# A new hand-written order for a fused attention and token-mixing kernel: narrow tiles for most q transposes and k'v products, and eps of 14 groups added by TensorE

## The chip, the cores and the metric

One core of a Trainium2 chip runs the whole kernel. The metric is device time in microseconds, the median of several runs. The profile is one further execution taken by the hardware profiler; its span runs from the first to the last instruction.

## What is computed

Linear attention with cosine weights, then a token mixer, for 8 batches, 8 heads, 576 tokens and head width 64, all inputs and the output in float32:

```python
r = np.maximum(x, 0.0)                                     # phi, for q and for k
phi = np.concatenate([r * c, r * s], axis=-1)              # c, s: cos and sin by token
kv = einsum('bhsf,bhsd->bhfd', k_p, v); z = sum(k_p, axis=2)
x = einsum('bhsf,bhfd->bhsd', q_p, kv) / (einsum('bhsf,bhf->bhs', q_p, z)[..., None] + 1e-06)
...
wq = x @ w_q; wk = x @ w_k                                 # x: 8 x 576 x 512, heads side by side
mixed = einsum('bst,btd->bsd', einsum('bsd,btd->bst', wq, wk) / 8, x)
out = np.maximum(mixed, 0.0) @ w_out
```

The kernel never forms the 576 x 576 token matrix: it computes wk'x (64 x 512) first and multiplies that by wq.

## The kernel before

The unit of the first half is H, one of 16: half a batch, four heads, as two pairs of heads. A step is a small function; its name is two letters and its number is H, a group g (two to an H), a batch b, or an output block. What happens to one H:

- LK, LQ, LV (line 145) load k, q and v from memory, mostly in two halves of 288 KB ("a" and "b", one per pair of heads), into rings of five raw buffers each. All loads and all stores are issued by SP, in the order written.
- RK and RQ (lines 203 and 205) take the relu and cast to bfloat16. V is scaled by the cosine and sine tables into buffer v2 (tiles named v) on one of two routes: VG (line 248) does it in one pass on POOL from the raw data; or CV (lines 209, 211, 213) casts it on some engine and VS (line 234) multiplies on DVE. Two v2 buffers exist, so that v of H waits for the k'v product of H-2.
- QT transposes q on PE. Wide (line 295) takes nine transposes of 128 x 128, narrow (line 301) eighteen of 64 x 64. QM then multiplies by the table on DVE: two instructions for wide (line 316), one for narrow (line 320). QT_WIDE names the H's that are wide.
- KV multiplies k by v2 on PE: wide (line 275) in eighteen matmuls, narrow (line 285) in thirty-six that use 64 x 64 tiles. KV_WIDE names the wide ones. KE copies the result out of PSUM (lines 209 or 213).
- N (line 340) multiplies q by k'v for a group g: numerator and denominator. The eps is added either by EP, on ACT (line 357) or DVE (line 359), or, for a group in EPS_PE, by two tiny matmuls (line 348); then RC reads the denominator straight from PSUM (line 378). RC or RJ (line 381) is the reciprocal, X (line 393) the division into x, on DVE.
- XT (line 406) or XR (line 419) transposes x on PE, with full or with half-height tiles, and XE copies it out.

The second half goes by batch b: WK, WQ, KX (lines 439, 452, 466), their copies KW, QW, XK, two copies of kx across partitions (XA, XB), the products MX (line 489) with relu ME (lines 500, 502). Two batches together give nine output blocks WO (line 509, four matmuls of 128 x 128 by 128 x 512), copied by OE into one of sixteen o buffers and stored by ST (line 519). The weights come by LW and are cast by CW.

Nothing schedules this at run time: ORDER, a string of words, is the program. A word is a step, with `@A`, `@V` or `@G` for the engine (ACT, DVE, POOL) and `:n` for its PSUM bank or its o buffer. Each engine works through its own words in the order written and waits where its data or its buffer is not ready. PSUM has eight banks, which the words share out. The loads of an H may run at most five H's ahead of the relus and the scaling.

Of the kernel before, what the change touches and what calls it, by code (L numbers as in the profile page):

```python
# [31 lines left out]
RC6 LQ4a KX0:4 X6 RK2@A QT2:2 RC7 X7 CV5@A KV2:0 LK7a XK0@V LV4a QM2 XB0@G QW0@A XT3:6 LV4b KE2@A
RK5@A LK4a VS5a N5:0 WU5:2 LK4b N4:2 VS5b XE3@A RQ5@G LV7a EP5@V KV5:4 RC5 RC4 X5 XA0@A LV7b X4
QT5:6 KE5@A RQ4@G LQ7b MX0:0 QM5 XR2:2 ME0@A LQ7a QT4:4 XE2@A LQ6a N10:0 QM4 MX1:6 CV4@G LK7b EP10@A
ME1@A WK1:2 LV6b WQ1:3 RC10 KW1@A VS4 RK4@A LQ6b KX1:2 MX2:6 LW2 N11:4 XK1@V QW1@A ME2@A EP11@V
KV4:2 LK6b RC11 XA1@G X10 CV7a@A CV7b@G LK6a X11 MX5:6 MX4:0 KE4@A RQ7b@G LV6a RQ7a@A VS7 N8:2 N9:4
ME5@A LV8a ME4@A QT7:6 RK7@G LW3 EP8@V EP9@V RJ4 RQ6a@A XT5:0 X8 LW4 XB1@G XE5@A X9 KV7:2 LW5 RQ6b@G
# [6 lines left out]
OE4:5@A KV8:0 QM8 XB2@A KV9:6 ST4 KE8@A LV12a MX9:4 KE9@A MX11:0 VG11a N16:2 ME9@A LK10a ME11@V
WQ3:6 RC16 LQ10b KX3:7 X16 QW3@A MX10:0 LV10a XK3@A N17:4 ME10@A N19:2 RK11@V N18:6 LV10b EP19@A
WO11:0 EP17@V RQ11@A LQ12a RC17 EP18@V X17 WO5:1 VG11b OE11:6@V WO10:4 OE5:5@A RC19 RC18 ST11 X18
WO9:5 LK12a X19 LK10b QT11:6 LQ13b OE9:7@A RQ10@G LV12b KV11:2 XA3@A QM11 XR8:0 LK12b KE11@A XR9:6
VG10a XE8@A QT10:2 LQ12b XE9@V WO0:5 QM10 OE10:8@A MX13:0 OE0:6@A MX12:6 N22:2 WO12:4 RQ13a@G ME12@V
EP22@A LV15a XB3@A ME13@A LV13a RC22 VG10b WK4:5 X22 LQ14b LV14b MX14:0 KW4@A N23:6 ME14@V LQ14a
MX15:2 EP23@A KX4:5 RK10@A LV13b WQ4:0 XK4@V RQ13b@G RC23 WO3:1 ME15@A X23 XA4@G XB4@A QW4@A RQ12b@G  # L50
KV10:2 OE3:9@V RQ12a@A QT13:6 OE12:10@A VG12 MX18:0 WO14:5 QM13 KE10@A ST12 ME18@A LK13b XR11:2
OE14:11@A LK13a MX16:0 N21:6 XE11@V ME16@A LV14a N20:4 EP21@A EP20@V RK12@A QT12:0 RJ10 X21 WO16:2
RQ14b@A X20 WO13:3 QM12 VG13 XR10:4 OE13:10@A MX19:6 KV12:0 ME19@A ST13 WO17:3 OE16:12@A LK15b
KE12@V XE10@V LK14b MX17:0 LK14a OE17:13@A N25:6 ME17@V N24:4 LV15b RQ14a@A WK5:3 ST2 EP25@V EP24@V
RK13@A RJ12 QT14:0 X24 WO21:2 KW5@A X25 CV14a@G KV13:4 OE21:10@A QM14 CV14b@A WQ5:3 ST21 KE13@A
# [6 lines left out]
ST14 XR15:0 ST6 MX25:4 MX27:6 XE15@V ME25@A WO22:3 ST23 ME27@V ST1 WK7:0 OE26:9@V ST24 MX24:6 KW7@A
MX26:4 WQ7:1 ME24@A ME26@V ST19 KX7:0 OE22:8@V ST26 WO28:2 XK7@A QW7@V ST22 XA7@G WO27:3 OE28:11@A
XB7@G ST28 MX31:0 MX28:4 MX30:6 ME31@V ME28@A WO29:2 ME30@A OE27:7@V MX29:4 OE29:4@V WO30:0 ME29@A
ST27 ST29 WO32:1 OE30:2@V WO33:4 ST30 OE32:9@V WO34:0 ST32 OE33:8@A WO35:1 ST33 OE34:7@V WO31:4 ST34
OE35:4@A ST35 OE31:2@A ST31
# [532 lines left out]
```

## Time and profile before

| | |
|---|---|
| runs | 119.72, 120.26, 120.61 us; median 120.26 |
| span of the profiled execution | 117.9 us, 4967 instructions |
| PE, DVE, ACT, POOL busy | 96.3, 91.0, 82.7, 64.8 us |
| moved by DMA | 39.38 MB, mean 334 GB/s over the span |
| loads | 96 of k, q and v, 6 of weights; 36 stores |

The profiled execution gives its span alone, so that is set beside the runs: 2.4 us of the median lie before the first and after the last instruction. Busy time counts a matmul to its modelled end, and matmuls overlap, so PE's 96.3 us is more than its queue's own pace needs. A row of a group reads: line, engine, operation, output and inputs with shapes, count, then busy time and mean length of one in ns, then idle time just ahead and what ended it. In the chain of waits a row is start, length, and what the time went to.

### The profile page before, as it was taken

How to read it: one execution, taken by the hardware profiler on the slowest of the kernel's cores; microseconds unless marked ns; L12 is line 12 of the kernel's file. 1: busy time of each engine (PE TensorE's matmuls, PEld its weight loads, DVE VectorE, ACT ScalarE, POOL GpSimd, SP SyncE). 2: the span in 40 equal slices, each digit the busy share in tenths (PEclk: the TensorE clock that was granted, in tenths of full speed). 3: DMA queues.
4: the chain of work that ended last, by engine and by line, in shares of the span. 5: the costliest groups of instructions: out<-in, count | busy, mean ns of one | idle time of the engine just before them, and what ended most of it. 6: DMA issues, size and time to landing. Idle time of an engine off the chain costs nothing.

```text
span 117.9 us, 4967 instructions
## 1 busy us (share of the span) xinstructions
PE 96.3 (82%) x2109; PEld 65.3 (55%) x2109; DVE 91.0 (77%) x163; ACT 82.7 (70%) x146; POOL 64.8 (55%) x66
## 2 busy tenths in 40 slices
PE   0007866887897879998999889997999999999970
PEld 0006855756676768546966556654784566463420
DVE  2009799699899998989798887796997996794620
ACT  4555578489999797997684769975888783546340
POOL 7600599843435984584599972899549921102000
PEclk9999999999999999999999999999999999999998
DMA  3999999999999999999999899786989456999874
GB/s 95 353 389 408 393 363 351 391 389 396 385 393 389 391 385 387 389 395 384 387 381 341 271 317 379 274 253 215 299 285 321 171 205 268 402 343 402 340 306 172
DMA packets 20662, 39.38 MB, mean 334 GB/s; under 512 B 3232, under 2 KB 3232, under 8 KB 20640
## 3 DMA queue, kind: packets, MB, share of 16 engines
q1 hardware_dynamic: 20640, 39.07, 91.8%
q8 instruction: 16, 0.26, 1.0%
q14 instruction: 6, 0.05, 0.1%
HBM read 29.62 MB, written 9.44 MB: 331 GB/s over the span
## 4 chain that ended last, share of the span: by engine, by line
PE 46%; DMA 25%; DVE 9%; SPq 8%; ACT 4%; issue 3%; POOL 2%; POOLq 0%; DVEq 0%
PE ps L509 23%; DMA kraw<-in_k_dram 11%; DMA vraw<-in_v_dram 9%; SPq L145 8%; DMA qraw<-in_q_dram 5%; DVE qm L316 5%; PE ps L340 4%; PE ps L452 3%; PE ps L466 3%; PE ps L489 3%; PE ps L439 3%; PE ps L285 3%; PE ps L419 2%; PE ps L295 2%; POOL rq L205 2%
## 5 line engine op out<-in xcount | busy, mean ns | idle before, releaser
L248 POOL TENSOR_TENSOR v<-vraw,vtab 128x1152 bf16<-128x1152 f32 (+1 forms) x12 | 35.6, 2976 | 4.5 <-DVE qm L316 2.5
L509 PE MATMUL ps<-wow,mix 128*128 128x512 bf16 x144 | 34.6, 380 | 0.0
L393 DVE TENSOR_TENSOR x<-ps,rec 128x640 bf16<-128x640 f32 x32 | 25.4, 816 | 0.7
L209 ACT COPY o<-ps 128x512 f32<-128x512 f32 x25 | 14.6, 590 | 10.5 <-PE ps L509 9.2
L316 DVE TENSOR_TENSOR qm<-ps,qtab 128x1152 bf16<-128x1152 bf16 x28 | 19.7, 749 | 1.3 <-PE ps L295 1.2
L509 PEld LDWEIGHTS <-mix 128*128 128x128 bf16 x144 | 12.5, 98 | 14.5 <-issue 1.7
L295 PE MATMUL ps<-ident,rq 128*128 128x128 bf16 x126 | 10.3, 232 | 10.9 <-ACT rq L203 10.0
L234 DVE TENSOR_TENSOR v<-vb,vtab 128x2304 bf16<-128x2304 bf16 (+1 forms) x11 | 12.0, 1110 | 7.5 <-ACT vb L209 6.7
L500 ACT ACTIVATE mix<-ps 128x576 bf16<-128x576 f32 x23 | 14.5, 651 | 2.5 <-PE ps L489 2.3
L340 PE MATMUL ps<-kvs,qm 64*128 64x65 bf16 x640 | 14.0, 193 | 2.8 <-DVE qm L316 1.8
L340 PEld LDWEIGHTS <-qm 64*128 64x128 bf16 x640 | 12.6, 96 | 4.9 <-issue 3.3
L295 PEld LDWEIGHTS <-rq 128*128 128x128 bf16 x126 | 8.2, 104 | 12.5 <-issue 9.9
L203 ACT ACTIVATE rk<-kraw 128x1152 bf16<-128x1152 f32 (+1 forms) x14 | 13.9, 995 | 0.5 <-DMA kraw<-in_k_dram 0.3
L211 POOL TENSOR_SCALAR kx<-kx 64x256 bf16<-64x256 bf16 x10 | 4.0, 400 | 15.8 <-ACT kx L209 10.1
L205 POOL TENSOR_SCALAR rq<-qraw 128x576 bf16<-128x576 f32 (+1 forms) x13 | 10.1, 776 | 4.4 <-ACT rk L203 2.6
L211 POOL TENSOR_SCALAR vb<-vraw 128x576 bf16<-128x576 f32 (+1 forms) x7 | 5.7, 809 | 10.8 <-DMA vraw<-in_v_dram 9.5
L285 PE MATMUL ps<-v,rk 64*64 64x130 bf16 x432 | 9.1, 228 | 1.9 <-ACT mix L500 0.7
L209 ACT CAST kvs<-ps 128x260 bf16<-128x260 f32 (+1 forms) x15 | 6.5, 436 | 5.1 <-PE ps L285 3.8
L285 PEld LDWEIGHTS <-rk 64*64 64x64 bf16 x432 | 7.5, 112 | 4.3 <-ACT mix L500 1.3
L502 DVE TENSOR_SCALAR mix<-ps 128x576 bf16<-128x576 f32 x9 | 6.8, 753 | 3.3 <-PE ps L489 3.1
L213 DVE COPY xT<-ps 128x1280 bf16<-128x1280 bf16 (+1 forms) x9 | 7.3, 813 | 2.2 <-PE ps L419 2.0
L203 ACT ACTIVATE rq<-qraw 128x576 bf16<-128x576 f32 (+1 forms) x10 | 8.3, 830 | 0.9 <-DMA qraw<-in_q_dram 0.8
(65 smaller groups left out, 135.0 us busy)
## 6 DMA issues: line engine op xcount, KB each, us to landing
kraw<-in_k_dram SPq DMA_DIRECT2D x32, 288.0 KB, 5.9
qraw<-in_q_dram SPq DMA_DIRECT2D x32, 288.0 KB, 5.9
vraw<-in_v_dram SPq DMA_DIRECT2D x32, 288.0 KB, 5.9
out_dram<-o SPq DMA_DIRECT2D x36, 256.0 KB, 3.0
wof<-in_moe_w_out_dram SPq DMA_DIRECT2D x4, 256.0 KB, 5.7
wkf<-in_moe_w_k_dram SPq DMA_DIRECT2D x1, 128.0 KB, 6.7
wqf<-in_moe_w_q_dram SPq DMA_DIRECT2D x1, 128.0 KB, 6.5
```

Of the source, the lines that this page charges most:

```text
L203: A.activation(dst, s, AF.Relu)
L205: eng.tensor_scalar(dst, s, FMAX, 0.0, op0=ALU.min, op1=ALU.max)
L209: A.copy(dst, s)
L234: V.tensor_mul(v2_b[H % NV2][:, part, :, :, 0:D], vb_b[H % NPREP][:, part].unsqueeze(3).to_broadcast([P, n, C, 2, D]), vtab.unsqueeze(1).t ...
L248: G.tensor_mul(dst[:, part, :, :, 0:D], s[:, part].unsqueeze(3).to_broadcast([P, n, C, 2, D]), vtab.unsqueeze(1).to_broadcast([P, n, C, 2, ...
L285: nc.tensor.matmul(kv_v[o, r, :], rk_of(H)[a, pr, c, :], v2_b[H % NV2][a, pr, c, :, 0:D + 1], start=(c == 0), stop=(c == C - 1))
L295: nc.tensor.transpose(qt_v[:, c, :], rq_b[H % NPREP][:, c, :, :], ident)
L316: V.tensor_mul(qm_b[H % NQM][:, :, r, 0:C, :], q_t[:, r].unsqueeze(1).to_broadcast([P, 2, C, H2]), qtab)
L340: nc.tensor.matmul(nv[:, pr, u, :], qm_b[H % NQM][a, s, r, 2 * u:2 * u + 2, :], kv_b[H % 2][a, r, pr if H in KV_WIDE else 0, s, 0:D + 1], ...
L393: V.tensor_tensor(x_b[b % NX][:, :, 4 * h:4 * h + 4, :].rearrange("p u (w r) d -> p r w u d", r=2)[:, r], nv[:, :, :, 0:D], rec(g).to_broa ...
L500: A.activation(dst, s, AF.Relu, scale=scale_moe)
L509: nc.tensor.matmul(o, mix_b[bp % 2][:, m, rt * P:(rt + 1) * P], wow[:, m, :], start=(m == 0), stop=(m == NDM - 1))
```

## The change

The ORDER string is replaced whole, and with it the three tables that name the tile forms and the eps groups. No step's function changes.

```diff
-    EPS_PE = (3, 4, 14, 16, 26)
+    EPS_PE = (0, 2, 4, 6, 8, 9, 10, 11, 12, 13, 15, 16, 17, 19)
...
-    QT_WIDE = (0, 1, 2, 3, 4, 5, 6, 7, 8, 9, 10, 11, 12, 14)
-    KV_WIDE = (2, 4, 5, 7)
+    QT_WIDE = (0, 1, 9)
+    KV_WIDE = (0, 1, 2)
...
-OE2:2@A WO4:2 LK11a VS9 OE6:3@A LQ11a RK8b@A QT9:0 RK9a@G OE1:4@A WK3:3 LV11b QM9 QT8:4 RK9b@G KW3@A
...
+LQ13b XB2@A KV8:4 VG10 OE0:6@A KE8@A LQ13a XT7:0 MX8:4 ME8@V QT9:2 XE7@A QM9 WO6:6 N16:0 OE6:7@A
```

The H's are now taken in order (0, 1, 2, 3, ...) where they went in swapped pairs (1, 0, 3, 2, ...). Step by step, before and now: wide q transposes 14 and 3 (narrow 2 and 13); wide k'v 4 and 3; EP on ACT 12 and 11, on DVE 15 and 7; groups with eps from PE 5 and 14; XT 4 and 5, XR 12 and 11; halves of v scaled by VG on POOL 15 and 23, by VS on DVE 17 and 9; halves of k relu on POOL 6 and 14, on ACT 23 and 15; of q on POOL 16 and 10, on DVE 3 and 10; the sixteen copies of kx (XA, XB) on POOL 10 and 1, on ACT 6 and 9, on DVE 0 and 6.

Three places. First, POOL's queue near its end; v20, v21 are the v2 buffers, vraw, kraw and qraw with a number the raw ones, rk, rq and vb the relus and the cast. Before:

```order
L205 TENSOR_SCALAR rq0_80<-qraw2_70 128x9x64
L248 TENSOR_TENSOR v20_84<-vraw2_75,vtab_125 128x36x64
L248 TENSOR_TENSOR v21_85<-vraw3_76,vtab_125 128x36x64
L211 TENSOR_SCALAR vb0_82<-vraw4_77 128x576
L205 TENSOR_SCALAR rk0_78<-kraw4_67 128x576
L211 TENSOR_SCALAR kx1_103<-kx1_103 64x256 x2
L248 TENSOR_TENSOR v21_85<-vraw0_73,vtab_125 128x18x64
L205 TENSOR_SCALAR rq1_81<-qraw0_68 128x9x64
```

Now:

```order
L248 TENSOR_TENSOR v21_85<-vraw3_76,vtab_125 128x18x64
L248 TENSOR_TENSOR v20_84<-vraw4_77,vtab_125 128x18x64
L248 TENSOR_TENSOR v21_85<-vraw0_73,vtab_125 128x18x64
L248 TENSOR_TENSOR v20_84<-vraw4_77,vtab_125 128x18x64
L205 TENSOR_SCALAR rq1_81<-qraw0_68 128x9x64 x2
L248 TENSOR_TENSOR v21_85<-vraw0_73,vtab_125 128x18x64
L205 TENSOR_SCALAR rk0_78<-kraw4_67 128x576
```

The scaling of v for H = 13, 14, 15 stands in halves close together, in turns between the two v2 buffers, with the second half of k of H = 14 behind it all.

Second, SP's queue around the first stores that stand among the loads (o buffers by number). Before:

```order
L145 DMA vraw3_76<-in_v_dram 128x576
L519 DMA out_0_dram<-o10_116 128x512
L145 DMA kraw3_66<-in_k_dram 128x576 x2
L145 DMA vraw4_77<-in_v_dram 128x576
L519 DMA out_0_dram<-o10_116 128x512
L145 DMA kraw0_63<-in_k_dram 128x576
```

Now:

```order
L145 DMA qraw4_72<-in_q_dram 128x576
L519 DMA out_0_dram<-o3_109 128x512
L145 DMA vraw4_77<-in_v_dram 128x576
L145 DMA qraw0_68<-in_q_dram 128x576
L519 DMA out_0_dram<-o1_107 128x512
L519 DMA out_0_dram<-o5_111 128x512
```

Before, a store follows its block's copy closely and the same o buffer comes twice with three loads between; now three stores of blocks that were copied long before stand at that place.

Third, DVE's queue where q of H = 2 and 3 is weighted. Before:

```order
L213 CAST kx0_102<-ps_122 128x256
L316 TENSOR_TENSOR qm0_86<-ps_122,qtab_126 128x2x576 x2
L234 TENSOR_TENSOR v21_85<-vb1_83,vtab_125 128x18x64 x2
L359 TENSOR_SCALAR rec2_92<-ps_122 128x10
L378 RECIPROCAL rec2_92<-rec2_92 128x10
```

Now:

```order
L320 TENSOR_TENSOR qm0_86<-ps_122,qtab_126 128x4x576
L320 TENSOR_TENSOR qm1_87<-ps_122,qtab_126 128x4x576
L359 TENSOR_SCALAR rec2_92<-ps_122 128x10
L378 RECIPROCAL rec2_92<-ps_122 128x10
L378 RECIPROCAL rec2_92<-rec2_92 128x10
```

One instruction per H in place of two, the scaling of v gone from between, and one eps addition fewer, its reciprocal reading PSUM.

More of the change, by code (lines that the diff above doesn't have):

```diff
@@ L32 @@
[L32 to L37, printed above, removed]
@@ L44 @@
[L44 to L49, printed above, removed]
@@ L50 @@
[L50 to L55, printed above, removed]
@@ L62 @@
[L62 to L66, printed above, removed]
+LQ0a LQ0b LV0a TB TK TQ TI TW LK0a LV0b LK0b LQ1b LV1a TV LV1b RQ0b@V RQ0a@V QT0:0 CV0b@V LK1a LK1b
@@ new lines @@
+OE9:10@V N20:4 ST12 XK4@V XA4@V RK11b@A WO17:0 WO13:1 CV12a@A RK11a@A QM11 KV11:2 EP21@A VG12b
+OE17:11@A OE13:12@A WQ4:0 EP20@V RJ10 KE11@A VS12a XB4@V X20 LV15b N22:2 RK12b@G X21 RK12a@G QW4@A
+RQ12b@A EP22@V RQ13@G N23:4 MX19:0 WO11:6 EP23@A WO16:7 RQ12a@A VS13b RJ11 ME19@A OE16:13@A QT12:0
+OE11:14@A X22 X23 KV12:2 XR11:4 QM12 XR10:6 KE12@A XE10@V WO14:2 VG13a MX18:0 MX16:6 VG14a XE11@A
+ME18@A QT13:4 ST7 LK15a LK14b WK5:3 ME16@A KW5@A RK13a@V N24:0 RK13b@V KV13:6 VG15a QM13 EP24@A
+KX5:3 OE14:15@A WQ5:2 RC24 X24 MX17:0 N25:4 QW5@V KE13@A XK5@A N26:6 EP25@V ME17@A N27:2 RC25 XA5@V
@@ L67 @@
+OE24:4@V XR15:6 XR14:0 ST24 MX24:2 OE25:11@A XE14@V XE15@A WO22:4 WK7:5 OE22:3@V ME24@A MX27:2
+ME27@V MX25:6 KW7@A ME25@A MX26:0 WQ7:4 KX7:5 ME26@A XK7@A XA7@G ST26 QW7@V WO28:6 XB7@V MX30:4
+MX29:0 ST22 ST14 MX28:2 ST25 WO27:7 OE28:2@V ME28@A ST10 ME30@A ST23 ST8 WO30:6 OE27:5@V MX31:4 ST27
+WO29:7 ME29@V ME31@V OE29:1@V WO32:0 ST28 WO35:1 WO34:7 WO33:4 WO31:5 OE30:14@A OE34:6@A OE32:9@V
+OE35:7@V ST29 ST32 ST30 ST35 ST34 OE33:10@A OE31:4@A ST33 ST31
 """
```

43 lines of the change are left out of this document (27 added, 16 removed).

## The prediction

> **What bounds the kernel now.** I read the page first, then the busy time by stage, then the chain of waits in order of time, then the waits of the SP queue. The first view, cut where the character of the chain changes:
>
> ```profile
> 0.00:31.00 31.00, 17.49 (x454) 14.16 (x454) 21.02 (x44) 20.56 (x31) 17.49 (x26) 1.00 0.99 354
> 31.00:54.00 23.00, 20.75 (x440) 14.94 (x441) 21.65 (x38) 20.97 (x39) 14.12 (x19) 1.00 1.05 390
> 54.00:77.00 23.00, 21.55 (x546) 15.23 (x544) 19.27 (x33) 17.28 (x35) 16.89 (x11) 1.00 0.96 337
> 77.00:114.30 37.30, 36.50 (x672) 20.99 (x671) 29.04 (x51) 23.32 (x43) 16.34 (x13) 1.00 0.82 294
> ```
>
> Columns: stretch, length, busy us of PE, PEld, DVE, ACT and POOL, PE clock, DMA share, GB/s. Up to 54 us the transfers run without a break at about 390 GB/s: loads set the pace, with DVE at 21.65 of 23 us close behind. From 54 us the DMA falls back, and from 77 us PE is busy 36.5 of 37.3 us. The clock is full in all four, so it is no term here. The chain says the same of the end:
>
> ```profile
> 73.30 0.66 POOL rq L205
> ...
> 76.43 0.57 ACT mix L500
> ...
> 80.00 0.66 ACT mix L500
> ...
> 82.59 0.62 PE ps L340 x40
> 83.21 0.69 PE ps L439 x20
> 83.90 0.50 PE ps L295 x9
> 84.40 0.86 PE ps L509 x4
> 85.26 0.65 PE ps L285 x35
> 85.91 0.69 PE ps L452 x8
> 86.60 0.55 PE ps L466 x10
> 87.15 0.40 PE ps L419 x20
> ...
> 92.37 0.24 PE ps L489 x4
> 92.62 0.97 PE ps L509 x4
> ...
> 94.31 0.26 PE ps L301 x18
> ...
> 103.38 0.58 PE ps L439 x20
> ...
> 108.98 5.30 PE ps L509 x24
> 114.30 0.58 ACT o L209
> ```
>
> From 80.67 us on each piece is PE work, one behind the other, until 114.28; then a copy, a store and the end of the span at 117.9, 3.6 us later. These pieces are the prices of PE's steps: what PE's queue moves on by, shorter than the mean of a single MATMUL suggests, since matmuls overlap.
>
> Between 73.3 and 77.0 the chain is POOL and ACT: load-driven work that came late. Why it was late stands in SP's waits and its timeline:
>
> ```profile
> SPq L519 <- ACT o L209: 10.5, 7, 3.0
> SPq L519 <- DVE o L213: 5.7, 6, 2.9
> ...
> 70.36 0.33 SPq L145 DMA_DIRECT2D vraw<-in_v_dram  x1
> 75.15 0.34 SPq L519 DMA_DIRECT2D out_dram<-o  x1
> ...
> 88.87 0.43 SPq L145 DMA_DIRECT2D kraw<-in_k_dram  x1
> ```
>
> SP issues in order. At 70.7 us it stood before a store whose block was not written until 75.15; the k, v and q loads behind it waited 4.5 us. The last load left at 88.87. So three things take turns: loads until about 54, a mixture with late loads until 77, PE alone after that.
>
> **The change, step by step.** The rows that price the moved work:
>
> ```profile
> L248 POOL TENSOR_TENSOR v<-vraw,vtab 128x1152 bf16<-128x1152 f32 x9 | 21.9, 2433 | 3.0 <-DVE qm L316 2.5 <-DMA vraw<-in_v_dram 0.4
> L205 POOL TENSOR_SCALAR rq<-qraw 128x576 bf16<-128x576 f32 x10 | 6.6, 665 | 1.2 <-DMA qraw<-in_q_dram 0.7 <-PE ps L509 0.2
> L205 POOL TENSOR_SCALAR rk<-kraw 128x576 bf16<-128x576 f32 x4 | 4.2, 1062 | 4.6 <-DMA kraw<-in_k_dram 4.6
> L211 POOL TENSOR_SCALAR kx<-kx 64x256 bf16<-64x256 bf16 x10 | 4.0, 400 | 15.8 <-ACT kx L209 10.1 <-DVE rec L378 2.4 <-DVE rec L359 1.9
> L234 DVE TENSOR_TENSOR v<-vb,vtab 128x2304 bf16<-128x2304 bf16 x6 | 8.4, 1406 | 0.7 <-POOL vb L211 0.7
> L234 DVE TENSOR_TENSOR v<-vb,vtab 128x1152 bf16<-128x1152 bf16 x5 | 3.6, 754 | 6.8 <-ACT vb L209 6.7
> L316 DVE TENSOR_TENSOR qm<-ps,qtab 128x1152 bf16<-128x1152 bf16 x28 | 19.7, 749 | 1.3 <-PE ps L295 1.2
> L320 DVE TENSOR_TENSOR qm<-ps,qtab 128x2304 bf16<-128x2304 bf16 x2 | 2.7, 1353 | 0.3 <-PE ps L301 0.3
> L359 DVE TENSOR_SCALAR rec<-ps 128x10 f32<-128x10 f32 x15 | 2.0, 152 | 1.6 <-PE ps L340 1.4 <-ACT rec L357 0.2
> L205 DVE TENSOR_SCALAR rq<-qraw 128x576 bf16<-128x576 f32 x1 | 0.7, 743 | 0.0
> L203 ACT ACTIVATE rk<-kraw 128x1152 bf16<-128x1152 f32 x9 | 10.4, 1160 | 0.5 <-DMA kraw<-in_k_dram 0.3
> 86.69 1.35 DVE L234 TENSOR_TENSOR v<-vb,vtab 128x2304 bf16<-128x2304 bf16 x1
> 87.09 1.46 POOL L205 TENSOR_SCALAR rk<-kraw 128x576 bf16<-128x576 f32 x1 [2.90 <-DMA kraw<-in_k_dram]
> ```
>
> *PE.* Eleven transposes of q go from wide (0.50 us) to narrow (0.26): 11 x 0.24 = 2.6 us less. The change also adds: nine more groups get their eps by two tiny matmuls each, a second warm matmul, one XT for an XR. None of these is over 0.3 us of queue time, together 0.6; one k'v product fewer is wide (bounded by the 0.65 of a narrow one, and taken as 0.2 less). A change of tile shape also costs: the 128-row product takes 0.97 behind a 64-row piece (92.62, behind MX) and 0.86 behind a 128-row transpose (84.40); WK 0.69 against 0.58. In the new order PE's tile shape changes 92 times, before 86, counted step by step: 6 x 0.11 = 0.7 us. Sum for PE: -2.6 + 0.6 - 0.2 + 0.7 = -1.5 us.
>
> [...] Counted in the order, most narrow transposes replace a switch that was there.
>
> Is the saving worth its 1.5 us? Seven of the eleven transposes lie before H=9, where loads set the pace, and count only if PE fills the gap. It does: before the k'v product of H=9 the new order has eight output products (WO), the old six. Their 0.9 us each no longer stand in the all-PE stretch at the end. I take the whole 1.5, bounds 0.6 (late transposes alone, less the switches) and 2.6.
>
> *DVE.* Scaling of v on DVE falls from 17 halves to 9 (12.0 to 6.8 us), eight eps additions go (1.1), eleven QM become one instruction (19.7/14 = 1.41 to 1.35, 0.6), two XE leave (1.6) and three XK (1.2). It gains relus of q (2 whole, 3 halves, 3.7 us by the 0.743 row), three QW (1.3), one output copy (0.7), two casts of v and six kx copies. The last two have no row on DVE: bounds 0.2 and 0.75 each, taken as 0.6 and 0.3, 3.0 together. Net about -1.5 us of 91 (the four stages' sum). ACT: eight whole k relus fewer (9.3), eight halves more (5.6), two v casts fewer, two XE and three XK more: about -4 of 82. Both are near the pace in the loaded stage, so I put 0.8 us of it on the path (bounds 0 and 2.0).
>
> *SP.* One row says how long loading takes to start:
>
> ```profile
> 7.40 1.15 ACT L209 CAST vb<-vraw 128x1152 bf16<-128x1152 f32 x1 [1.04 <-DMA vraw<-in_v_dram]
> ```
>
> The new order issues five stores before the last load, the old seven, and each long after its block's copy. The old order's 4.5 us stop goes. What it cost is the non-PE part of the chain, 73.30 to 77.05 and 80.00 to 80.66, 4.4 us, of which PE filled most with products; I take 1.2, bounds 0 and 4.4. With unbroken loading at 390 GB/s, the 30.9 MB up to the last load are there at 30.9/0.391 + 3.6 = 82.7 us (3.6 is the start: ACT's wait above ended at 7.4 us with five loads, 1.47 MB, and 1.47/0.391 = 3.8).
>
> *POOL.* This is what the change pays with. Scaling of v goes from 15 halves to 23: 8 x 2.4 = 19 us. Eight more halves of k at 0.66 to 1.06 (6), six fewer of q and six fewer casts of v (7 less), nine fewer kx copies (3.6 less), two weight casts more (1): +15 us, 64.8 to about 80. POOL must then work nearly without a gap from 12 us until the last k is in. At the end its queue holds, behind k'v of H=13: two halves of v, two of q, one of v, one of k: 3 x 2.4 + 2 x 0.67 + 0.7 to 1.5 = 9.2 to 10.0 us before k'v of H=14 can start. PE has between the two: six products (5.3), three N at 0.31, one k'v 0.65, two transposes 0.26, two XR 0.40, WK, WQ, KX (1.9), three MX (0.4) = 10.5 us. A margin of half a us to a us, and none for waits. POOL slows when DVE works out of SBUF beside it: the k half that ran beside L234 at 87.09 took 1.46 us, others 0.66. I charge +0.8, bounds 0 and 6.
>
> [...]
>
> Sum: -1.5 - 0.8 - 1.2 + 0.8 = **-2.7 us**, so a span of 115.2 from 117.9. The median of the runs shown, 120.26, lies 2.4 above the span; what lies around it stays, giving **117.5 us**, 2.2% less. A measurement of this kernel tells about 1% from no change.
>
> **The rivals.** *POOL becomes the bound (slower).* Place: POOL's queue from VG10 to the k relu of H=14. Price: its own work ends at the earliest at 86 us (6 us until the first half of v is in, 76 us of work without the setup, 4 us of gaps while the first loads come); the PE work behind k'v of H=14 is about 20 us and the tail 3.6, so 110. Each us of waiting or slowing adds directly once the slack of about 4 to 5 us is gone. It turns into a loss when POOL loses over 10 us in 74: waits like the 15.8 us before kx or the 4.6 before rk now, or ten operations drawn out as at 87.09. Then 122. For: +15 us on one engine in order; against: most of those old waits were for late data that loads now bring sooner. [...]
>
> *The PE saving is hidden (same).* If POOL delivers v too late for the extra two products to fit early, only the four late transposes count, 1.0 us, less switches 0.7, and the store waits show as waits elsewhere: 120.0. *Relief adds up (faster still).* If late loads cost all of the 4.4 us and DVE's 2.0 lie on the path, and POOL keeps up: -1.5 - 2.0 - 4.4 = -7.9, at most half of it in practice beside PE's own work: about 115.
>
> **Chances.** Forecast 0.45, faster still 0.13, hidden 0.24, POOL bound 0.18. The range 114.3 to 121.8 leaves out the far ends of the last two; the forecast's own range is 116 to 119. Faster by over 1% (under 119.06): 0.58; within 1%: 0.24; slower: 0.18.
>
> **What would show it.** Right: L301 groups about 13 x 18 at 0.26 us a step in the chain; POOL near 80 us busy and over 90% between 15 and 80 us; SP's longest waits for a store before the last load under 1 us, the last load issued before 80 us; PE's last product ending near 111.5 with an all-PE chain from about 60 us on. Wrong: PE gaps that end on POOL v or POOL rk; SP loads waiting on POOL v (buffers not free); a late chain of ACT and DVE in the last 10 us in place of products.

## The result, and the profile after

The changed kernel takes 130.76 us (median of six runs, 126.13 to 134.44), the kernel before 120.16 us beside it on the same chip: a ratio of 1.055, 95% interval 1.048 to 1.063. Every ratio here leaves out runs over 1.5% above the fastest of their kernel, which the medians take in, so a loss reads smaller by its ratio (here 6.7 us) than by its median (10.6). Predicted were 117.5 us, with 114.3 to 121.8 as the range. The profiled execution has a span of 132.7 us where the one of before had 117.9; it was the longest of the six (134.44 us).

Its page, busy time by engine, then the granted TensorE clock and the DMA rate in forty slices:

```profile
PE 100.2 (76%) x2219; PEld 66.5 (50%) x2235; DVE 107.2 (81%) x155; ACT 78.8 (59%) x146; POOL 80.7 (61%) x66
...
PEclk9999999995999999997579999986999999999999
...
GB/s 133 330 388 400 365 376 373 396 387 388 370 377 399 376 385 392 388 391 390 370 377 334 348 333 327 291 15 23 219 5 0 0 136 397 339 109 401 298 348 206
```

POOL and ACT stand where they were forecast (about 80 us and some 4 us less than before). DVE doesn't: it should have lost 1.5 us of 91 and has gained 16. By stage (columns as in the prediction):

```profile
31.00:54.00 23.00, 18.18 (x472) 12.86 (x471) 22.68 (x27) 14.51 (x26) 21.30 (x19) 0.94 1.04 383
54.00:77.00 23.00, 18.82 (x434) 12.48 (x438) 20.09 (x27) 14.35 (x28) 16.53 (x9) 0.85 1.03 367
77.00:100.00 23.00, 18.72 (x502) 12.74 (x503) 20.80 (x28) 13.91 (x29) 13.70 (x9) 0.93 0.47 167
```

The transfers now run at 383 and 367 GB/s, near the 390 of before, until 77 us and somewhat beyond. The gain on before is in the third stage alone, 367 GB/s for 337, and is small: by 77 us 27.9 MB have moved, before 27.5. PE does less in every stage. SP's timeline and its longest wait:

```profile
79.83 1.07 SPq L145 DMA_DIRECT2D kraw<-in_k_dram  x2
```

```profile
SPq L519 <- ACT o L209: 25.1, 5, 13.5
```

The last two loads leave at 79.83 and 80.3 us (before: 88.87), and the stop of 13.5 us stands behind them. The last load left 8.5 us sooner, as meant, its data were there 4.9 us sooner (87.75 us, before 92.67), and that bought nothing.

What fills DVE is the length of single instructions. The groups, shapes kept apart:

```profile
L234 DVE TENSOR_TENSOR v<-vb,vtab 128x1152 bf16<-128x1152 bf16 x9 | 15.6, 1733 | 0.1
L213 DVE COPY kx<-kx 64x256 bf16<-64x256 bf16 x6 | 6.6, 1107 | 0.9 <-ACT kx L209 0.7
L205 DVE TENSOR_SCALAR rq<-qraw 128x1152 bf16<-128x1152 f32 x3 | 4.7, 1568 | 0.0
```

The first was 754 ns before; a kx copy that stands alone in this trace takes 0.22 us; for the whole relu of q before had one row:

```profile
L205 DVE TENSOR_SCALAR rq<-qraw 128x1152 bf16<-128x1152 f32 x1 | 0.8, 755 | 0.0
```

The excess of these three groups: 9 x 0.98 + 6 x 0.89 + 3 x 0.81 = 16.6 us, as much as DVE gained. Where it comes from is seen by laying DVE's timeline beside POOL's. DVE:

```profile
45.09 2.86 DVE L234 TENSOR_TENSOR v<-vb,vtab 128x1152 bf16<-128x1152 bf16 x1
47.87 1.34 DVE L320 TENSOR_TENSOR qm<-ps,qtab 128x2304 bf16<-128x2304 bf16 x1
49.14 2.66 DVE L234 TENSOR_TENSOR v<-vb,vtab 128x1152 bf16<-128x1152 bf16 x1
...
55.37 2.46 DVE L205 TENSOR_SCALAR rq<-qraw 128x1152 bf16<-128x1152 f32 x1
57.74 2.92 DVE L234 TENSOR_TENSOR v<-vb,vtab 128x1152 bf16<-128x1152 bf16 x1
...
60.82 1.56 DVE L393 TENSOR_TENSOR x<-ps,rec 128x640 bf16<-128x640 f32 x2
```

POOL in the same stretch (the last row is two instructions, 54.83 to 60.05):

```profile
44.96 2.37 POOL L248 TENSOR_TENSOR v<-vraw,vtab 128x1152 bf16<-128x1152 f32 x1
48.79 2.38 POOL L248 TENSOR_TENSOR v<-vraw,vtab 128x1152 bf16<-128x1152 f32 x1 [1.46 <-PE ps L285]
...
54.83 5.22 POOL L248 TENSOR_TENSOR v<-vraw,vtab 128x1152 bf16<-128x1152 f32 x2 [0.62 <-PE ps L285]
```

Each long instruction of DVE begins while POOL scales v, and ends 0.6 us behind POOL's end (47.95 behind 47.33, 51.80 behind 51.17, 57.83 behind 57.20, 60.66 behind 60.05). Fifteen of DVE's instructions of these kinds that begin beside a POOL instruction end a fixed time behind it: 0.6 us the scaling and the whole relu of q, 0.3 the cast of half a v and the half relu of k, 0.08 the kx copy. So each seems to do its work, or the last part of it, only when POOL is through. The division that reads PSUM, L393, keeps its 0.82 us (at 14.77 and 17.51, beside POOL from 14.44 to 19.13). One form on SBUF isn't held either, the half relu of q; it takes 0.74 us for 576 elements where the whole one takes 0.755 for 1152, so it runs at half the whole one's pace. One half relu of k, at 12.41, isn't held: it takes 0.75 us (0.45 without POOL beside it) and ends 0.17 us ahead of POOL. Why these escape isn't shown:

```profile
10.96 2.37 POOL L248 TENSOR_TENSOR v<-vraw,vtab 128x1152 bf16<-128x1152 f32 x1
11.18 0.74 DVE L205 TENSOR_SCALAR rq<-qraw 128x576 bf16<-128x576 f32 x1
```

A POOL scaling keeps its 2.36 to 2.38 us where it begins first. Where DVE's begins first, POOL's waits in turn:

```profile
31.16 1.58 DVE L234 TENSOR_TENSOR v<-vb,vtab 128x1152 bf16<-128x1152 bf16 x1
32.09 2.87 POOL L248 TENSOR_TENSOR v<-vraw,vtab 128x1152 bf16<-128x1152 f32 x1
```

Over the whole trace that comes to about 4 us on POOL (nine instructions, 0.2 to 0.6 us each), against 16.6 on DVE. So the 16.6 us are waiting, inside the instruction. The chain of waits agrees: from 32.94 to 61.66 us it is DVE, but for 4 to 5 us that it calls issue, some of them inside held instructions. What it does to PE:

```profile
57.88 0.44 PE L301 MATMUL ps<-ident,rq 64*128 64x64 bf16 x18 [0.19 <-DVE rq L205]
61.70 1.19 PE L285 MATMUL ps<-v,rk 64*64 64x130 bf16 x36 [3.39 <-DVE x L393]
```

The k'v product of H=8 needs the bank that the division at 60.82 empties, and that stood behind both held instructions. PE is idle for 3.4 us, and in small windows of this execution the clock (the third column from the right) then falls:

```profile
60.00:61.50 1.50, 0.00 (x0) 0.00 (x0) 1.50 (x4) 0.00 (x0) 0.04 (x1) 0.86 1.05 392
61.50:63.00 1.50, 1.30 (x38) 1.13 (x38) 1.50 (x3) 0.07 (x1) 0.00 (x0) 0.50 1.05 389
...
66.00:67.50 1.50, 1.36 (x16) 0.52 (x17) 0.96 (x2) 0.26 (x1) 1.50 (x1) 0.50 1.04 370
67.50:69.00 1.50, 1.50 (x50) 1.22 (x46) 0.97 (x2) 1.16 (x3) 1.35 (x3) 0.86 1.06 392
```

At half the clock the four matmuls of an output product start 0.43 us apart in place of 0.22.

So two suspects at once, DVE held beside POOL and the clock; a third, PE's instruction supply, came out of the first experiments.

### The profile page after: what moved, and what is told of

The parts are those of the page before. It is cut to its first block, busy times and chain, and to the rows that moved or that the text cites. A ratio compares the mean times of both kernels' runs of the same rounds, so it can differ in the third digit from the quotient of the medians.

```text
span 132.7 us, 5206 instructions
## 1 busy us (share of the span) xinstructions
PE 100.2 (76%) x2219; PEld 66.5 (50%) x2235; DVE 107.2 (81%) x155; ACT 78.8 (59%) x146; POOL 80.7 (61%) x66
## 4 chain that ended last, share of the span: by engine, by line
PE 38%; DVE 32%; DMA 14%; issue 8%; ACT 3%; SPq 2%; DVEq 0%; ACTq 0%
PE ps L509 16%; DMA qraw<-in_q_dram 9%; DVE x L393 7%; DVE v L234 6%; DVE qm L320 5%; DMA kraw<-in_k_dram 5%; PE ps L285 3%; DVE kx L213 3%; DVE rq L205 3%; PE ps L340 3%; PE ps L489 3%; PE ps L406 3%; PE ps L466 2%; PE ps L439 2%; SPq L145 2%
## 5 line engine op out<-in xcount | busy, mean ns | idle before, releaser
L248 POOL TENSOR_TENSOR v<-vraw,vtab 128x1152 bf16<-128x1152 f32 (+1 forms) x21 | 55.5, 2650 | 21.0 <-PE ps L285 8.4
L393 DVE TENSOR_TENSOR x<-ps,rec 128x640 bf16<-128x640 f32 x32 | 25.6, 821 | 0.9
L320 DVE TENSOR_TENSOR qm<-ps,qtab 128x2304 bf16<-128x2304 bf16 x13 | 17.4, 1346 | 1.8 <-PE ps L301 1.7
L234 DVE TENSOR_TENSOR v<-vb,vtab 128x1152 bf16<-128x1152 bf16 x9 | 15.6, 1733 | 0.1
L205 POOL TENSOR_SCALAR rk<-kraw 128x576 bf16<-128x576 f32 (+1 forms) x12 | 10.7, 905 | 2.0 <-DMA kraw<-in_k_dram 1.7
L203 ACT ACTIVATE rk<-kraw 128x576 bf16<-128x576 f32 (+1 forms) x14 | 10.1, 721 | 2.7 <-DMA kraw<-in_k_dram 2.6
L209 ACT COPY xT<-ps 128x1280 bf16<-128x1280 bf16 (+1 forms) x9 | 10.7, 1191 | 1.6 <-PE ps L406 0.8
L213 DVE COPY o<-ps 128x512 f32<-128x512 f32 x12 | 8.2, 687 | 2.4 <-PE ps L509 2.0
L205 DVE TENSOR_SCALAR rq<-qraw 128x576 bf16<-128x576 f32 (+1 forms) x7 | 7.6, 1097 | 2.4 <-DMA qraw<-in_q_dram 2.4
L489 PE MATMUL ps<-wq,kx 64*128 64x288 bf16 x64 | 8.1, 297 | 0.7 <-DVE x L393 0.3
L295 PE MATMUL ps<-ident,rq 128*128 128x128 bf16 x27 | 3.4, 311 | 5.8 <-DVE rq L205 5.8
```

The lines of the kernel that those rows point to most:

```text
L205: eng.tensor_scalar(dst, s, FMAX, 0.0, op0=ALU.min, op1=ALU.max)
L209: A.copy(dst, s)
L213: V.tensor_copy(dst, s)
L234: V.tensor_mul(v2_b[H % NV2][:, part, :, :, 0:D], vb_b[H % NPREP][:, part].unsqueeze(3).to_broadcast([P, n, C, 2, D]), vtab.unsqueeze(1).t ...
L248: G.tensor_mul(dst[:, part, :, :, 0:D], s[:, part].unsqueeze(3).to_broadcast([P, n, C, 2, D]), vtab.unsqueeze(1).to_broadcast([P, n, C, 2, ...
L320: V.tensor_mul(qm_b[H % NQM][:, :, :, 0:C, :].rearrange("p s r c d -> p s r (c d)"), qt_view(place["QT", H]).unsqueeze(1).to_broadcast([P, ...
```

## The experiments

**The parts of the change alone.** The kernel before with the new tile tables and nothing else:

```diff
-    QT_WIDE = (0, 1, 2, 3, 4, 5, 6, 7, 8, 9, 10, 11, 12, 14)
-    KV_WIDE = (2, 4, 5, 7)
+    QT_WIDE = (0, 1, 9)
+    KV_WIDE = (0, 1, 2)
```

> The order and the eps groups of before, with the new tables of tile forms alone (11 q transposes and one k'v product narrow). Port theory (DVE held back by POOL is what costs the time): POOL's share is that of before, so DVE stays at 90 to 92 us and the time is 118 to 120. Tile theory (narrow tiles slow PE or lower its clock): 122 or more, granted clock under 0.98. POOL-queue theory: as the port theory, 118 to 120.

123.67 us, ratio 1.020 (1.006 to 1.033). PE was busy 94.8 us, 1.5 less than before, and the kernel lost 3.6 us (2.4 by the ratio). That the prediction's sum for PE has the same figure is chance: that sum had 1.3 us of losses that the tables alone don't bring (eps products, more changes of tile shape), so for the tables it had counted on 2.8. The first pause in PE's timeline, and all pauses without a releaser:

```profile
31.33 0.38 PE L301 MATMUL ps<-ident,rq 64*128 64x64 bf16 x14
33.08 0.24 PE L301 MATMUL ps<-ident,rq 64*128 64x64 bf16 x4 [1.37 <-issue]
```

```profile
PE ps L301 <- issue: 2.3, 2, 1.4
PE ps L340 <- issue: 2.2, 2, 1.3
PE ps L466 <- issue: 0.8, 1, 0.8
```

PE stops inside one step, after 14 of 18 transposes, with all data there. The five pauses make 5.3 us; 5.3 less 1.5 is 3.8, about the loss of this execution (123.8 us). Counting PE's matmuls and weight loads in the trace from zero, they stand at instructions 961, 1217, 1473, 1729 and 3521: 193 plus a multiple of 256, each time. The DMA records have a queue for instructions: 17 packets, 0.28 MB, on the page of the changed kernel, so 16 KB each, for 17 such places in PE's 4454 instructions; on the page of before 16 packets, 0.26 MB, for 16 places in 4218. So a packet seems to hold 256 instructions. A narrow step has twice the instructions of a wide one.

The opposite, the new order with the old tile tables:

```diff
-    QT_WIDE = (0, 1, 9)
-    KV_WIDE = (0, 1, 2)
+    QT_WIDE = (0, 1, 2, 3, 4, 5, 6, 7, 8, 9, 10, 11, 12, 14)
+    KV_WIDE = (2, 4, 5, 7)
```

> The new order and eps groups, with the tile tables of before. Port theory: DVE's operations out of SBUF are still held back by about 18 us in all, DVE busy over 103 us, time 125 to 132 as with the whole change. Tile theory: 119 to 122, clock 0.99. POOL-queue theory: 125 to 132.

132.83 us, ratio 1.100 (1.088 to 1.111): so the order carries the larger loss, and the narrow tiles, bad in the old order, are a gain in the new one (1.055 with them).

The third part, eps, in the old order (without groups 8 and 9; ten EP words go):

```diff
-    EPS_PE = (3, 4, 14, 16, 26)
+    EPS_PE = (0, 2, 3, 4, 6, 10, 11, 12, 13, 14, 15, 16, 17, 19, 26)
```

> The kernel before with its eps for ten more groups by two tiny matmuls each, ten additions on VectorE and ScalarE less (groups 8 and 9 are left as they were, since their reciprocal is one instruction for both): the third part of the change alone. Adds 20 matmuls (40 instructions) to TensorE, 0.6 us. By the instructions' theory: 120.3 to 121.3. By my prediction's pricing (0.5 us on TensorE, 1.1 us off VectorE, of which some pays): 119.5 to 120.3.

125.14 us, ratio 1.036 (1.030 to 1.042), from twenty tiny matmuls that should have been even. Nearly all of it is one place. PE, then ACT:

```profile
48.40 0.45 PE L419 MATMUL ps<-ident,x 64*128 64x64 bf16 x20
51.00 3.26 PE L509 MATMUL ps<-wow,mix 128*128 128x512 bf16 x10 [2.15 <-ACT vb L209]
```

```profile
50.21 0.67 ACT L209 CAST vb<-vraw 128x576 bf16<-128x576 f32 x1
```

The profile names the instruction of ACT that ended last, but the output product reads neither v nor its buffer: the name is a coincidence, and the matmul at 51.00 is again number 1729. From 52.50 to 55.50 the clock is then at 0.50.

**VectorE beside GpSimd.** Four edits of the changed kernel and one of the old. First, all 18 casts, relus and kx copies that the new order gives to DVE moved to ACT (`RQ8@V` becomes `RQ8@A`, and so on):

> The new order whole, but all relus, casts of v and kx copies that stand on DVE (18 words) are given to ACT at the same place; on DVE only the scaling of v still works from SBUF to SBUF. POOL's work is unchanged. Port theory: of the 18 us that DVE is held back half go (the scaling of v keeps some 9), DVE busy 86 to 92 us, time 118 to 124. Tile theory: 125 to 132, unchanged. POOL-queue theory: 125 to 132, unchanged, since POOL's 80 us and its waits for k'v stay.

129.07 us, ratio 1.070 (1.061 to 1.079). Here the port theory's number failed: by the ratio the kernel is slower than the changed one. DVE's busy time fell by 19 us, to 88.3, and that bought nothing, so DVE's busy time as such isn't what sets the time. The scaling of v stayed on DVE and stayed held, and ACT took the moved work beside its own (88.9 us). The scalings in its trace:

```profile
L234 DVE TENSOR_TENSOR v<-vb,vtab 128x1152 bf16<-128x1152 bf16 x9 | 14.6, 1619 | 8.7 <-ACT vb L209 8.5 <-POOL vb L211 0.2
```

Second, POOL's scaling cut short (this leaves out 56 of the 64 columns of v's scaling from H=4 on, where POOL does it):

```diff
-        if H in VG_SPLIT:
+        if H >= 4:
+            G.tensor_mul(dst[:, part, :, :, 0:8],
+                         s[:, part, :, 0:8].unsqueeze(3).to_broadcast([P, n, C, 2, 8]),
+                         vtab[:, :, :, 0:8].unsqueeze(1).to_broadcast([P, n, C, 2, 8]))
+        elif H in VG_SPLIT:
```

> The new order whole, but from H=4 on POOL scales only 8 of v's 64 columns and leaves the rest out, so each of these operations is short and POOL does some 30 us less. Port theory: DVE back to about 90 us busy, 114 to 119. POOL-queue theory: the same. Tile theory: 124 or more, since PE's work is unchanged.

124.45 us, ratio 1.032 (1.023 to 1.041): 6.3 us come back by the medians, 2.8 by the ratios, with DVE at 90.3 us and the scaling on DVE at 781 ns. The rest doesn't; six pauses at every 256th instruction, 6.9 us in all, stand in this trace in its place. This removes POOL's work as well as the holds, so it doesn't tell a queue on POOL from a hold. The next two do: the same work of POOL in two, then in four instructions.

```diff
-    VG_SPLIT = ()
+    VG_SPLIT = (0, 1, 2, 3, 4, 5, 6, 7, 8, 9, 10, 11, 12, 13, 14, 15)
```

> The changed kernel with each of GpSimd's scalings of v cut into its two tables' halves, two instructions of about 1.2 us in place of one of 2.4: the same elements. Port theory in its strict form (a VectorE instruction on SBUF that begins beside a GpSimd instruction is held until that one ends, so the loss goes with the length of GpSimd's single instruction): VectorE's busy time falls from 107 to 96 to 101 us, scaling of v by halves on VectorE from 1733 to 1300 ns or less, 125 to 128.5 us. In its loose form (the two share the port, each slowed as long as both work): VectorE stays at 105 or more, and the time at 129.5 or more.

125.65 us (four runs, 122.16 to 128.81; they scatter too much for an interval). The page and two groups, of the shortest run:

```profile
PE 96.9 (81%) x2235; PEld 63.7 (53%) x2235; DVE 96.7 (80%) x155; ACT 78.7 (65%) x146; POOL 84.5 (70%) x87
```

```profile
L234 DVE TENSOR_TENSOR v<-vb,vtab 128x1152 bf16<-128x1152 bf16 x9 | 9.9, 1095 | 0.5 <-ACT vb L209 0.4
...
L213 DVE COPY kx<-kx 64x256 bf16<-64x256 bf16 x6 | 4.1, 677 | 0.8 <-ACT kx L209 0.7
```

```diff
             for t in range(2):
-                G.tensor_mul(dst[:, part, :, t, 0:D], s[:, part], ...)
+                for x in (slice(0, 5), slice(5, C)):
+                    G.tensor_mul(dst[:, part, x, t, 0:D], s[:, part, x], ...)
```

> The changed kernel with each of GpSimd's scalings of v cut into four instructions, by table and by five and four of the nine blocks (two gave 125.7 us, one 130.8). Strict port theory: a hold ends with the GpSimd instruction beside it, now 0.6 to 0.7 us long, so VectorE's busy time falls from 97 to 91 to 94 us and scaling of v by halves on VectorE to 1000 ns or less; by the dose so far (one piece to two saved 10.5 us of VectorE and 5 us of time), 122 to 124.5 us, and not below 121.5, since the pauses at packets stay. If two pieces helped only by the place of the packets, 125 or more. If GpSimd's cost of each instruction decides: POOL busy over 92 us and 126 or more.

125.09 us, ratio 1.025 (1.020 to 1.030), with these groups and pauses:

```profile
L234 DVE TENSOR_TENSOR v<-vb,vtab 128x1152 bf16<-128x1152 bf16 x9 | 9.5, 1058 | 1.6 <-ACT vb L209 1.5
...
L213 DVE COPY kx<-kx 64x256 bf16<-64x256 bf16 x6 | 2.2, 366 | 0.9 <-ACT kx L209 0.7
```

```profile
PE ps L286 <- issue: 2.9, 2, 1.6
PE ps L302 <- issue: 1.4, 1, 1.4
...
PE ps L349 <- issue: 1.2, 1, 1.2
PE ps L341 <- issue: 0.5, 1, 0.5
```

POOL does the same work, and more of it by the clock (80.7, 84.5, 90.5 us busy); DVE's falls all the same (107.2, 96.7, 95.2), the kx copy by a step each time (1107, 677, 366 ns). The hold goes with the length of POOL's single instruction, as the strict theory has it; the third point missed the theory's bounds, by 1.2 us for DVE's busy time, by 58 ns for the scaling and by 0.6 us for the time. That median, 125.09, lies also where the rival (the place of the packets) had put it, at 125 or more; what speaks for the holds is the length of the instructions. In the trace of the changed kernel fifteen DVE instructions end 0.08 to 0.6 us behind the POOL instruction that they began beside, and the three POOL scalings that began second take 2.83 to 2.89 us in place of 2.37 and end 2.2 us behind DVE's instruction. What holds them no run here shows, nor why a few half relus escape. What is left over before, 4.9 us (3.0 by the ratio), has the size of the 6.0 us of pauses, all five at packets of 256.

The same cut in the old kernel, where POOL scales 15 halves in place of 23:

> The kernel before with the same cut of GpSimd's scalings of v. Strict port theory: VectorE's holds there are few (91 us busy, some 2 to 4 of it held), so 118.8 to 119.9 us, a little faster, unless TensorE paces it. Loose form: no change, 119.6 to 120.6. If the cut itself costs GpSimd time: 120.5 or more.

120.26 us, ratio 0.998 (0.995 to 1.002): nothing to win there. The strict theory's 118.8 to 119.9 was missed. In the trace of before the holds are small (the whole scaling 1.41 us against 1.35 alone), so there was little for the cut to bring back.

**The clock.** Matmuls that compute nothing ahead of PE's two long waits, so that the clock stays up:

```diff
-KV8:4
+WU74:2 KV8:4
...
-N23:4
+WU66:2 N23:4
```

> The changed kernel with matmuls that compute nothing ahead of its two long waits of TensorE: 18 ahead of the k'v products of H=8 (waits from 58.2 to 61.7 us), 16 ahead of the products of group 23 (83.9 to 87.0), on a free bank that a later step overwrites. TensorE stays busy up to about half a us before the waits end. Clock theory (the two waits bring the clock to a half for 6.8 and 3.2 us, so about 5 us of TensorE's time, on the chain): granted clock 0.98 or more, 125.5 to 128.5 us. Port theory alone (VectorE's queue sets the pace there, and a fast TensorE waits for it): clock up but 129.5 or more.

138.34 us. The second fill wrote a bank that still held the products of group 22, so this run changes part of the computation and says nothing of the clock. With `WU66:0` in its place:

> The changed kernel with matmuls that compute nothing ahead of TensorE's two long waits, 18 ahead of the k'v products of H=8 and 16 ahead of the products of group 23, the second now on a bank that holds nothing live (in the earlier run they destroyed the products of group 22 and waited for them to be read, which made that run worthless as a test of the clock). Clock theory: granted clock 0.98 or more, 125 to 128.5 us. Port theory alone: clock up, but 129.5 or more.

132.43 us, ratio 1.104 (1.099 to 1.109). The clock theory's 125 to 128.5 did not come; nor did its condition, a granted clock of 0.98 (the five runs had 0.969 to 0.987, the profiled one 0.974). In the profiled execution the clock was full from 54 to 100 us, where it had been 0.85 and 0.93, but the half clock near 31 us, which the changed kernel has too (30.4 to 33.8 us), was longer, 31.9 to 38.8. In all the half clock lasted 6.8 us, in the changed kernel's profile 13.7. The clock by slices:

```profile
PEclk9999999998559999999999999999999999999999
```

So filling these two waits doesn't pay, and half as much half clock went with no shorter time. Whether the clock costs something of its own in the changed kernel stays open.

**The packets of instructions.** First, matmuls of two columns, as many as the narrow tiles would add, at the same places of the old kernel; and a control of like length in few instructions:

```diff
+    def WD(i, ps, eng):
+        n, shape = divmod(i, 4)
+        rows, cols = ((H2, H2), (H2, P), (P, P), (P, H2))[shape]
+        for _ in range(n):
+            nc.tensor.matmul(bank(ps)[0:cols, 0:2], wc[0:rows, WARM_COLS:WARM_COLS + cols],
+                             wc[0:rows, 0:2], start=True, stop=True)
...
-QT2:2
+WD38:2 QT2:2
```

> The kernel before, its tiles unchanged, with instructions of almost no length added to TensorE's queue: 9 matmuls of two columns (18 instructions with their weight loads) ahead of each transpose step of q for H=2 to 12, 18 of them (36 instructions) ahead of the k'v products of H=4, 5 and 7, which is what the narrow tiles add at the same places. They write the bank that the step behind them overwrites; the output is the reference's. Fetch theory (TensorE's instructions come in packets of 256, one in 5.5 us at best while loads run, so an instruction costs time even where TensorE has time): 122 to 125 us, and pauses of 1 to 2 us without a wait at every 256th instruction between 26 and 60 us. Tile theory (narrow tiles themselves and their changes of shape cost): 120 to 121, no more than the run with one matmul of the same length.

> The control: the kernel before with one matmul of 384 columns (2 instructions) ahead of each transpose step of q for H=2 to 12, and two ahead of the k'v products of H=4, 5 and 7: TensorE is busy for about as long as with the many short ones (17 x 0.16 = 2.7 us in all), but issues 34 instructions more in place of 306. Fetch theory: 120 to 121.3, no pauses. Tile theory: 120 to 121.3 too, and the run with many equal to it.

The many: 123.61 us, 1.028 (1.024 to 1.033). The few (`WU6:2 QT2:2`): 122.35 us, 1.019 (1.016 to 1.023), a us more than I had expected of it. The time of the many is about as expected, its mechanism isn't: pauses of 1 to 2 us at every 256th instruction were forecast, and its trace has two at packets, 0.27 and 0.63 us. Nor are the tiny matmuls free; nine of them move PE's queue on by 0.24 us, which makes about 4 us for all 153:

```profile
56.44 0.37 PE L555 MATMUL ps<-warm 128*128 128x2 bf16 x9
56.67 0.66 PE L295 MATMUL ps<-ident,rq 128*128 128x128 bf16 x9
```

So the pair tells less than it should: 306 instructions cost 1.1 us more than 34 by the ratios, most or all of which their own length explains, and in the profile of the 34 (the longest of its runs, 125.22 us) there is a pause of 2.56 us before instruction 1729, the place of the eps run.

That suggested that the number of instructions matters less than where each packet of 256 begins. The trace records when PE enters a packet, when the next is moved, and when PE reaches it. For the one due at instruction 1729 (us; one execution each; the third column is the start of the last instruction ahead of it):

```
                enters 1473   packet moved     before 1729   1729 starts
before          44.88         48.37 to 49.45   50.95         50.96
34 shifted      44.66         46.72 to 47.81   48.02         49.08
eps             45.40         48.52 to 49.55   48.66         51.00
few (control)   45.68         49.69 to 50.73   49.67         52.23
eps, 200 more   41.76         44.05 to 45.15   48.14         48.19
```

The packet seems to be asked for when PE enters the one before it: in these five traces its move begins 2.1 to 4.0 us later, while loads run, and takes 1.0 to 1.1 us. Where PE waits, it goes on 1.3 to 1.5 us after the packet has landed, 4.4 to 6.6 us after it entered the one before; the 5.5 and 5.9 us of the expectations are estimates of that. In the kernel before, PE needs it 1.5 us after its landing, so it comes just in time. With 34 to 40 instructions more ahead of it, the packet that PE is working through then holds mostly short instructions (products, transposes), is used up in 3.3 to 4.0 us, and PE waits.

The test: tiny matmuls at the very start, in the 9 us in which PE has nothing to do. No work is added where the kernel works; all boundaries shift.

```diff
-LK1b TB TI
+LK1b TB WD68:6 TI
```

> The kernel before with 17 matmuls of two columns (34 instructions) at the very start of TensorE's queue, in the 9 us in which it waits for the first data: no work is added where the kernel works, only the place of each later instruction in the packets of 256 moves by 34. Packet theory (a packet is asked for when the one ahead of the running one is entered and is usable some 5.9 us later under load; a stretch of short instructions that fills one packet runs dry): in the trace of before the boundary at 44.9 us moves to 44.4 and the next packet is due 2.5 us too late; 121.8 to 123.5 us, with a pause of about 2 us at TensorE's instruction 1729. Any theory by work, waits or tiles: 119.6 to 120.7, no change.

121.37 us, ratio 1.011 (1.007 to 1.014). The pause is where it was forecast, though half as long, inside one transpose step; with another of 0.56 us at 25.64 it makes 1.4 us, the size of the loss (1.3 by the ratio):

```profile
47.76 0.45 PE L419 MATMUL ps<-ident,x 64*128 64x64 bf16 x19
49.09 0.20 PE L419 MATMUL ps<-ident,x 64*128 64x64 bf16 x1 [0.88 <-issue]
```

With 240 instructions (`WD480:6`):

> The same with 120 such matmuls (240 instructions) at the same place, seven times as many: the boundaries come to lie 16 instructions from where they were (240 is 256 less 16). Packet theory: 119.8 to 121.2, since no boundary comes to a stretch that runs dry by over 0.8 us. If padding itself costs by its number of instructions: 123 or more.

121.61 us, ratio 1.012 (1.008 to 1.016): 0.4 us outside what I had expected. No pause of over 0.7 us stands at a packet in its trace. The first transpose starts at 9.94 us, before at 9.49, which is a third of the loss; where the rest lies stays open, and padding may cost something of its own. And the padding on the eps run (`WD400:6`):

> The kernel before with ten more groups of eps on TensorE (125.1 us when run alone), and 100 matmuls of two columns (200 instructions) at the start of TensorE's queue. Packet theory: the pause of 2.3 us at instruction 1729 and the half clock behind it go, 119.8 to 121.8 us. If the eps products cost by their work or by later reciprocals: 124 to 126 as without the padding.

121.71 us, ratio 1.004 (1.000 to 1.008). With all the work of the eps run and 200 instructions more, 3.4 us come back by the medians, 3.8 by the ratios, though five of the eleven runs took 122.8 to 124.2 us. That is the clearest of these runs: by itself the eps part costs about half a us; it had moved the packets.

In the trace of the kernel before no wait of PE is put down to issue; pauses of 1 to 7 us in all stand in the traces of most of the variants.

**Smaller questions.** Narrow transposes only where PE runs alone (`QT_WIDE` = 0 to 9, so H=10, 11, 12 and 14 are added):

> The kernel before, narrow transposes of q added only where TensorE runs alone: H=10, 11, 12 and 14 (with 13 and 15, which were narrow). Saves 4 x 0.24 = 1.0 us of TensorE and adds 72 instructions behind 63 us. Fetch theory: 119.0 to 120.2, since packets come faster than they are used up there. Tile theory (the loss of 3.6 us with eleven narrow transposes and one more narrow k'v is spread over them): 120.8 to 121.8.

120.69 us, ratio 1.005 (1.002 to 1.008). No pause to speak of, and no gain of a us either; the time lies in neither range that I had given. And the other way, all transposes wide (`QT_WIDE` = 0 to 15):

> The kernel before with the two last narrow transposes of q, H=13 and 15, wide as well: 36 instructions fewer behind 74 us and 2 x 0.24 us more on TensorE, and qm of these H written by two instructions of 0.75 us, the first of which releases the first products, in place of one of 1.35. My prediction's pricing (TensorE alone paces the end): 120.4 to 121.0. Latency theory (narrow transposes late, which lost 0.5 per cent in place of winning 0.8, lose because their products wait 0.6 us longer for qm): 119.4 to 120.1.

120.84 us, ratio 1.004 (1.001 to 1.007). The latency theory falls with that. This one lies in the range that the prediction's prices gave, the one before doesn't; why neither pays is open. Last, the new order with POOL's scaling short (the same part is left out as above) and the old tiles:

> The changed kernel with GpSimd's scaling of v cut to 8 of 64 columns from H=4 on (so part of v's scaling is left out) and with the wide and narrow tiles of before. Fetch and port theories together (VectorE stretched beside GpSimd is the one cause, packets of instructions the other, 4.4 us over before were left with the first taken away): 118 to 121 and no pauses at packets. Order theory (the new order of the steps is itself worse, apart from both): 123 or more.

122.33 us, ratio 1.020 (1.017 to 1.024): by the ratios 9.6 us better than with POOL's scaling whole, 1.4 better than with narrow tiles, and not level with before. Pauses were forecast to vanish and didn't: five of 0.3 to 0.9 us at packets, 2.6 us in all. The order theory's 123 was not reached either: what is lost over before, 2.4 us, is no more than the pauses, so a loss that is the order's own isn't shown.

## Why the prediction was wrong

**PE, -1.5 us.** The term counted work, and the sign was right: busy time fell by 1.5 us with the tables alone, where the terms that belong to them had promised 2.8. The step that failed is "I take the whole 1.5": it turned PE's work into time without asking whether PE's instructions are there. In the old order the tables cost 3.6 us (2.4 by the ratio), in a trace with 5.3 us of such pauses. In the changed kernel itself this is not the larger error: its trace has one pause at a packet, of 1.5 us at 28.9, about as much as the whole term, and against the wide ones (1.055 and 1.100) the narrow tiles are a gain in its order.

**The eps products.** Priced with the second warm matmul and an XT at "together 0.6". With the packets put back they cost 0.5 us by the ratio, padding included; where they shift a packet, 4.3.

**DVE and ACT, -0.8 us.** The largest error. I took 0.743 and 0.754 us for the relus and the scaling of v from rows in which POOL was mostly idle (64.8 of 118 us), and put them into an order in which POOL is hardly ever idle in the loaded stage (21.3 of 23 us). The step that failed was to price each of these from such rows and forecast DVE at -1.5 us net; it measured +16.2 busy, 16.6 of it waiting beside POOL. (The term's own items add up to -1.0, not -1.5; that is not what failed.) The half relus of q kept 0.745, beside POOL too; the whole ones took 1.57, the scaling 1.73, the kx copy 1.11 on the mean. The size of the kx copies was bounded by 0.2 and 0.75; the bound was too low, since a held instruction lasts until POOL's ends, up to 2.34 us here.

**SP, -1.2 us.** Right in mechanism: loads with hardly a break, the last issued at 80.3 us (forecast: before 80). Their data were there at 87.75 us, 5 us later than the 82.7 forecast, since the stages ran at 383 and 367 GB/s up to 77 us and at 167 after it. It won nothing; the chain of waits was on DVE before that.

**POOL, +0.8 us, and the first rival.** Busy 80.7 us, as forecast, about 4 us of it waiting beside DVE. The prediction had one row of POOL beside DVE and read it one way: "POOL slows when DVE works out of SBUF beside it". It went the other way in most places. The row at 87.09 us was a POOL instruction that had begun second; here POOL's come first, are three times as long, and DVE waits. The rival's sign was right, its place (POOL's queue behind VG10) and its price (122) were not: cutting POOL's instructions, with more POOL time, brought 5.7 us back by the medians, 3.6 by the ratios.

**The clock, "no term here".** True of before, not of after: 0.949 over the span of its profiled execution. What it costs by itself the fills didn't settle.

**The range.** 121.8 was drawn from the rivals that I had. All of them moved the bound between engines; only POOL's charge let an instruction's price change with its neighbour, and none did so for DVE or asked for PE's instructions.

## What to carry to other kernels

Take an instruction's price from rows that had the same neighbours: where a change fills POOL, allow for each SBUF instruction of DVE to last until the POOL instruction it meets ends (fifteen did here, a scaling of 0.75 us up to 2.92; the half relus of q and one half relu of k did not), and keep POOL's instructions short. Count PE's instructions as well as its work, and look for "issue" pauses at equal distances of 256: an edit can lose 3% by where the packets begin (1.036 and 1.004 for the same eps products), and padding ahead of the first data tells that from the edit itself. When a change loses by two causes, taking one away shows the next; price them one at a time before adding them up.

## What the runs showed of the hardware

- Fifteen VectorE instructions on SBUF that began beside a GpSimd one ended a fixed time after GpSimd's end (0.6 us the scaling and the whole relu of q, 0.3 a cast or half relu of k, 0.08 a copy): a copy of 0.22 us took 2.34. The half relus of q, 0.74 us, were not held, nor was one half relu of k (0.75 us). A GpSimd scaling that began first kept its 2.37 us; one that began second waited as well and took 2.87.
- TensorE's instructions come 256 at a time: 17 packets of 16 KB for 17 such places in the changed kernel, 16 for 16 in the one before. With transfers at 386 to 394 GB/s a packet that PE waited for was usable 4.4 to 6.6 us after PE had entered the one before it, and 1.3 to 1.5 us after it had landed.
- Of two pauses of TensorE between 2 and 2.5 us one was followed by half the clock: behind the 2.34 us of the eps run it was 0.50 from 52.50 to 55.50 us, behind the 2.49 us before 52.45 in the changed kernel it stayed at 1.00 until 60 us.
